# Gate and value of a GEGLU block by row parity: one block in three of the last sixty with one TensorE pass less, doubled even parts on ScalarE and sums on POOL

## Chip, cores, metric

One core of one Trainium2 chip. The metric is the device time of one execution in microseconds (us). A single-core program has no second die to compare with, so the state of a run is judged by its time against the fastest of the same kernel. Kernel times are medians. Where a ratio stands, it is the mean time of one kernel's fast runs over that of the other kernel's fast runs of the same rounds, so not quite the ratio of the medians that are quoted.

## The reference

```python
X = np.fft.fft(np.fft.fft(x, axis=1), axis=2).real        # x: 8 x 3008 x 256
x = X.reshape(24064, 256)
gelu = 0.5 * g * (1 + erf(g / sqrt(2)))   # g = x @ w_gate      (256 x 1536)
out  = (gelu * (x @ w_val)) @ w_out       #                     (1536 x 256)
```

Row t and row T - t of the transform are even and odd combinations of the same numbers. The kernel therefore holds an even part E and an odd part O for half the rows only, and makes "forward" rows from E + O and "mirrored" rows from E - O. The lowest odd channel is zero by nature; its place in O carries another number y, which belongs to the even side and needs a correction in the mirrored rows.

## The kernel before: the parts that matter

A *block* is one 128-wide slice of the hidden layer for up to 512 pairs of rows. There are 8 batches x 3 chunks x 12 slices = 288 blocks, numbered 0 to 287. Chunks have 512, 512 and 481 pairs. The last batch (252 to 287) has no later batch's transform beside it; its own is made beside blocks up to 249.

```python
def psum(tag):
    bufs = {"g": 2, "v": 3, "o": 1, "dft": 2}[tag]     # 8 banks in all
    return psum_pool.tile([128, 512], FP32, tag=tag, bufs=bufs, name=f"ps_{tag}")

# gate, forward rows: E + O, then GELU on ScalarE
mm(pg, n, "g", "E", fs, E, True, False)
mm(pg, n, "g", "O", fs, O, False, True)
nc.scalar.activation(gl[:, 0, :n], pg[:, :n], AF.Gelu)
# gate, mirrored rows, a block later: a third pass adds -2 O into the same bank
mm(pg, n, "g", "M", fs, O, False, True, skip_group_check=True)
nc.scalar.activation(_sub(gl, [[-1, n]], TOK + n - 1), pg[:, :n], AF.Gelu)

# value: two passes; VectorE keeps the even part (plus y * yw) before the second
mm(pv, n, "v", "E", fs, E, True, True)
nc.vector.scalar_tensor_tensor(ve[:, :n], EB_bufs[b][:, c0 : c0 + n],
    yw[:, fc : fc + 1], pv[:, :n], op0=ALU.mult, op1=ALU.add)
# ... a block later
mm(pv, n, "v", "O", fs, O, False, True, skip_group_check=True)
nc.vector.tensor_tensor(st["h"][:, fc, 0, :n], gl[:, 0, :n], pv[:, :n], op=ALU.mult)
nc.vector.scalar_tensor_tensor(_sub(vv, [[-1, n]], n - 1), ve[:, :n], 2.0, pv[:, :n],
    op0=ALU.mult, op1=ALU.subtract)                     # mirrored = 2 E' - (E + O)
nc.gpsimd.tensor_tensor(st["h"][:, fc, 1, :n], gl[:, 1, :n], vv[:, :n], op=ALU.mult)
# [...]
# per block, in every engine's queue in this order ("before" is the previous block):
parts["G"][fc]()                        # gate, forward
before[0]["g"][before[1]]()             # gate, mirrored
parts["V"][fc]()                        # value, even
two.pop(0)()                            # four output matmuls of the chunk before
before[0]["v"][before[1]]()             # value, odd, and the products
two.pop(0)()                            # four more; every third block ends with
                                        # ScalarE's copy of ps_o to out_sb
```

Two facts carry the whole argument: every engine takes its operations in the order of this listing (the traces below show a copy that is ready at 558.28 and starts at 559.08, behind a GELU queued ahead of it), and there are two gate banks and one output bank.

## Time and profile before

| | before |
|---|---|
| time, median (lowest to highest) | 629.23 us (628.73 to 629.72, 4 runs) |
| span of the profiled run | 627.0 us |
| busy: TensorE, VectorE, ScalarE, POOL | 98%, 92%, 68%, 81% |
| three blocks in the pure stretch (252 to 275, no transform work beside them) | 5.86 us |

In the profile PE is TensorE, PEld its weight loads, DVE VectorE, ACT ScalarE, and POOL the fourth compute engine. The prediction below shows the lines of the profile and how it reads them. In a line of the instructions in order of time the columns are start, duration, engine, source line, operation, output and inputs, shapes; in brackets stands the idle time of the engine just before, and whose end ended it. A matmul's recorded 0.38 us is its latency; its pace is 0.217.

### The profile page before, as it was taken

Reading aid. Unit: us, or ns where it says so; the run is one execution under the profiler, and the core shown is the slowest. Engines: PE = TensorE matmul, PEld = TensorE weight load, DVE = VectorE, ACT = ScalarE, POOL = GpSimd, SP = SyncE. Lnnn points to the kernel's source line nnn. Section 1 sums busy time; section 2 is a strip of 40 time slices with the busy share of each in tenths; the row PEclk is TensorE's granted clock in tenths of the full one; section 3 lists DMA queues with packets and bytes.
Section 4 is the critical chain, followed back from the end, with each engine's and each line's share of the span. In section 5 each row is a group of like instructions: output and inputs, shape, how many; then the busy total and the mean of one; then the engine's idle time right before and its main releaser. Section 6 shows DMA issues by size and latency. Waiting matters only on the chain.

```text
span 627.0 us, 12895 instructions
## 1 busy us (share of the span) xinstructions
PE 612.3 (98%) x4195; PEld 405.1 (65%) x4243; DVE 578.3 (92%) x941; ACT 428.4 (68%) x842; POOL 505.3 (81%) x510
## 2 busy tenths in 40 slices
PE   7999999999999999999999999999999999999997
PEld 3456666666666666666666666666666666666666
DVE  8689989999899999999999998999999999999992
ACT  6777677666776677667676677676676666666661
POOL 8399999989897998879997899969988655555651
PEclk8999999999999999999999999999999999999999
DMA  9961754536353353731645335633212322221123
GB/s 177 227 97 31 210 129 116 144 105 159 99 146 101 98 133 79 184 113 46 160 110 135 101 78 127 148 97 98 62 49 63 91 86 55 51 52 39 42 51 81
DMA packets 54217, 65.40 MB, mean 104 GB/s; under 512 B 7831, under 2 KB 49802, under 8 KB 51754
## 3 DMA queue, kind: packets, MB, share of 16 engines
q1 hardware_dynamic: 47222, 49.03, 30.6%
q0 software_dynamic: 6608, 15.29, 11.4%
q8 instruction: 33, 0.54, 0.4%
q10 hardware_dynamic: 320, 0.26, 0.2%
q14 instruction: 34, 0.28, 0.2%
HBM read 39.65 MB, written 30.17 MB: 111 GB/s over the span
## 4 chain that ended last, share of the span: by engine, by line
PE 93%; ACT 2%; issue 1%; DVE 1%; DMA 1%; POOL 1%; POOLq 0%; ACTq 0%
PE ps_o L749 38%; PE ps_g L660 28%; PE ps_v L660 19%; PE ps_dft L546 2%; PE ps_dft L582 2%; PE ps_o L820 1%; DMA Z_sb<-z 1%; PE ps_dft L443 1%; PE ps_dft L612 0%; ACT gelu_sb L676 0%; POOL h_sb L724 0%; POOL eo_sb L224 0%; DMA out_dram<-out_sb 0%; ACT gelu_sb L685 0%; PE ps_dft L749 0%
## 5 line engine op out<-in xcount | busy, mean ns | idle before, releaser
L724 POOL TENSOR_TENSOR h_sb<-gelu_sb,v_sb 128x512 bf16<-128x512 bf16 (+1 forms) x280 | 319.8, 1146 | 93.1 <-DVE v_sb L722 85.9
L749 PE MATMUL ps_o<-Wo_sb,h_sb 128*128 128x256 bf16 (+1 forms) x2232 | 334.9, 273 | 0.9 <-POOL h_sb L724 0.9
L749 PEld LDWEIGHTS <-h_sb 128*128 128x128 bf16 (+1 forms) x2304 | 228.7, 100 | 112.9 <-POOL h_sb L724 2.6
L676 ACT ACTIVATE gelu_sb<-ps_g 128x512 bf16<-128x512 f32 (+1 forms) x288 | 169.4, 588 | 98.6 <-PE ps_g L660 80.9
L660 PE MATMUL ps_g<-EO_sb,W_sb 128*128 128x512 bf16 (+1 forms) x817 | 228.5, 375 | 3.8 <-ACT gelu_sb L685 0.8
L704 DVE SCALAR_TENSOR_TENSOR ve_sb<-EB_sb,yw,ps_v 128x512 f32<-128x512 bf16 (+1 forms) x280 | 206.3, 737 | 25.9 <-PE ps_v L660 25.0
L660 PE MATMUL ps_v<-EO_sb,W_sb 128*128 128x512 bf16 (+1 forms) x575 | 213.7, 375 | 0.7 <-DVE W_sb L451 0.6
L720 DVE TENSOR_TENSOR h_sb<-gelu_sb,ps_v 128x512 bf16<-128x512 bf16 (+1 forms) x280 | 189.9, 678 | 1.1 <-ACT gelu_sb L685 0.7
L660 PEld LDWEIGHTS <-W_sb 128*128 128x128 bf16 x1440 | 137.2, 98 | 81.1 <-issue 1.8
L722 DVE SCALAR_TENSOR_TENSOR v_sb<-ve_sb,ps_v 128x512 f32<-128x512 f32 (+1 forms) x280 | 187.5, 670 | 0.0
L685 ACT ACTIVATE gelu_sb<-ps_g 128x512 bf16<-128x512 f32 (+1 forms) x288 | 168.7, 586 | 0.0
L769 ACT ACTIVATE out_sb<-ps_o 128x512 f32<-128x512 f32 x92 | 55.0, 598 | 35.7 <-PE ps_o L749 35.6
L224 POOL TENSOR_TENSOR eo_sb<-ab_sb 94x512 bf16<-94x512 f32 (+1 forms) x70 | 77.6, 1111 | 0.5
L549 ACT ACTIVATE S_sb<-ps_dft 96x512 bf16<-96x512 f32 x56 | 32.9, 588 | 14.0 <-PE ps_dft L546 13.9
L592 ACT ACTIVATE EO_sb<-ps_dft 128x512 bf16<-128x512 f32 (+1 forms) x44 | 26.0, 590 | 23.3 <-PE ps_dft L582 22.1
L217 POOL TENSOR_TENSOR ab_sb<-x_raw,x_raw 94x508 f32<-94x508 f32 (+1 forms) x30 | 33.0, 1100 | 0.0
L220 POOL TENSOR_TENSOR ab_sb<-x_raw,x_raw 94x508 f32<-94x508 f32 (+1 forms) x30 | 32.9, 1098 | 0.0
L546 PE MATMUL ps_dft<-eo_sb,G 94*96 94x256 bf16 x119 | 22.5, 274 | 0.2 <-POOL eo_sb L224 0.2
L158 POOL DMA_INDIRECT x_raw<-in_x_dram,idx x18 | 17.1, 948 | 2.9 <-issue 1.1
L582 PE MATMUL ps_dft<-TP,Z_sb 128*128 128x128 bf16 (+1 forms) x184 | 17.8, 218 | 0.0
L582 PEld LDWEIGHTS <-Z_sb 128*128 128x128 bf16 x192 | 14.6, 98 | 1.8 <-DVE Z_sb L534 0.6
L546 PEld LDWEIGHTS <-G 94*96 94x96 bf16 x119 | 13.0, 123 | 1.2 <-issue 0.4
(148 smaller groups left out, 166.2 us busy)
## 6 DMA issues: line engine op xcount, KB each, us to landing
out_dram<-out_sb SPq DMA_DIRECT2D x364, 64.0 KB
x_raw<-in_x_dram SPq DMA_DIRECT2D x10, 768.0 KB
Z_sb<-z SPq DMA_DIRECT2D x7, 768.0 KB
z<-S_sb SPq DMA_DIRECT2D x7, 576.0 KB
EB_sb<-yrow SPq DMA_DIRECT2D x14, 128.0 KB
z<-S_sb SPq DMA_DIRECT2D x7, 192.0 KB
x_raw<-in_x_dram SPq DMA_DIRECT2D x2, 640.0 KB
EB_sb<-yrow SPq DMA_DIRECT2D x7, 120.2 KB
```

The lines of the kernel that those rows point to most:

```text
L224: eng.tensor_tensor(_sub(eo, [[C, nj], [1, 128]], j0 * C + g * 128), ab(0, 0, [[1, 128]]), ab(1, 0, [[1, 128]]), op=op)
L546: nc.tensor.matmul(ps[:96, q * C : (q + 1) * C], G[:, j, :], _sub(eo, [[1, C]], j * C), start=(j == js[0]), stop=(j == js[-1]))
L582: nc.tensor.matmul(ps[:, o : o + n], st["Z"][:, pair, g * 128 : g * 128 + 128], _sub(TP, [[1, n]], g * 128), start=True, stop=True)
L660: nc.tensor.matmul(ps[:, :n], W[nm, part][:, fs], src, start=start, stop=stop, **kw)
L676: nc.scalar.activation(gl[:, 0, :n], pg[:, :n], AF.Gelu)
L685: nc.scalar.activation(_sub(gl, [[-1, n]], TOK + n - 1), pg[:, :n], AF.Gelu)
L704: nc.vector.scalar_tensor_tensor(ve[:, :n], EB_bufs[b][:, c0 : c0 + n], yw[:, fc : fc + 1], pv[:, :n], op0=ALU.mult, op1=ALU.add)
L720: nc.vector.tensor_tensor(st["h"][:, fc, 0, :n], gl[:, 0, :n], pv[:, :n], op=ALU.mult)
L722: nc.vector.scalar_tensor_tensor(_sub(vv, [[-1, n]], n - 1), ve[:, :n], 2.0, pv[:, :n], op0=ALU.mult, op1=ALU.subtract)
L724: nc.gpsimd.tensor_tensor(st["h"][:, fc, 1, :n], gl[:, 1, :n], vv[:, :n], op=ALU.mult)
L749: nc.tensor.matmul(pso[:m, half], st["h"][:, fc, sign, h0 : h0 + m], Wo_sb[:, fc, :], start=(fc == 0 and not (first and sign)), stop=(fc = ...
L769: nc.scalar.activation(_sub(osb, [[1, 2 * C]], 0, part_num=m), pso[:m, :], AF.Copy)
```

## The change

The intent: spare the third gate pass. In a treated block the gate is done like the value. ScalarE copies the doubled even part out of the bank before the odd pass is added, VectorE forms y * 2w - (E + O), POOL adds the two, and ScalarE takes GELU of that. The value half is changed too, because VectorE has no room for one more operation: its "keep the even part" is replaced by another doubling on ScalarE and another sum on POOL. Treated are blocks 229, 232, ... 283, which are 19.

```diff
+    APART = tuple(i for i in range(B * NS - 60, B * NS - 2) if i % 3 == 1)
 # l1_gate
+                if apart(ci, fc):
+                    mm(pg, n, "g", "E", fs, E, True, True)
+                    nc.scalar.activation(e2[:, :n], pg[:, :n], AF.Copy, scale=2.0)
+                    return
 # l1_gate_odd, new: queued behind the block's first four output matmuls
+                mm(pg, n, "g", "O", fs, O, False, True, skip_group_check=True)
+                nc.vector.scalar_tensor_tensor(
+                    d[:, :n], EB_bufs[b][:, c0 : c0 + n], ywg[:, fc : fc + 1], pg[:, :n],
+                    op0=ALU.mult, op1=ALU.subtract)
+                nc.scalar.activation(gl[:, 0, :n], pg[:, :n], AF.Gelu)
+                nc.gpsimd.tensor_tensor(d[:, :n], e2[:, :n], d[:, :n], op=ALU.add)
+                st["ps"][fc][0] = d
 # l1_gate2: the mirrored GELU reads d, without the third pass
 # l1_value
+                    nc.scalar.activation(e2[:, :n], pv[:, :n], AF.Copy, scale=2.0)
 # l1_value2
+                    nc.vector.scalar_tensor_tensor(
+                        _sub(vv, [[-1, n]], n - 1), EB_bufs[b][:, c0 : c0 + n],
+                        yw2[:, fc : fc + 1], pv[:, :n], op0=ALU.mult, op1=ALU.subtract)
+                    nc.gpsimd.tensor_tensor(vv[:, :n], _sub(ve, [[-1, n]], n - 1), vv[:, :n], op=ALU.add)
+                    nc.gpsimd.tensor_tensor(st["h"][:, fc, 1, :n], gl[:, 1, :n], vv[:, :n], op=ALU.mult)
 # make_ywg, new, in block 14: four small matmuls and copies, and
+        nc.vector.tensor_scalar(yw2, yw, 2.0, None, op0=ALU.mult)
 # [...]
```

More of the change, by code (lines that the diff above doesn't have):

```diff
@@ L135, in v_tile, with e2_tile @@
         return work([128, TOK], FP32, "v", 4, "v_sb")
+    def e2_tile():
+        return work([128, TOK], FP32, "e2", 2, "e2_sb")
     def osb_tile():
@@ L245 @@
     one_h = const_pool.tile([1, 1], BF16)
-    yw = const_pool.tile([128, NFC], FP32)
+    yw, yw2, ywg = (const_pool.tile([128, NFC], FP32, name=f"yw_{i}") for i in range(3))
     NGP = NJ * NK
@@ L477, in make_yw, with make_ywg @@
         return run
+    def make_ywg():
+        fcs = sorted({i % NFC for i in APART})
+        ps = psum("dft")
+        for fc in fcs:
+            nc.tensor.matmul(
+                ps[:, fc : fc + 1], W["g", "O"][0:1, fc * 128 : (fc + 1) * 128], one_h, start=True, stop=True)
+        for fc in fcs:
+            nc.scalar.activation(ywg[:, fc : fc + 1], ps[:, fc : fc + 1], AF.Copy, scale=2.0)
+        nc.vector.tensor_scalar(yw2, yw, 2.0, None, op0=ALU.mult)
     EO_bufs, EB_bufs = {}, {}
@@ L634, in tp_o @@
         return tp_e(b, gi, 1, engine)
+    NS = NG * NFC
+    APART = tuple(i for i in range(B * NS - 60, B * NS - 2) if i % 3 == 1)
     def store(b, gi, sub, sign, osb_half, queue):
@@ L667, in cols_of, with apart @@
             return n, c0, E, O, cstate[ci], slice(fc * 128, (fc + 1) * 128)
+        def apart(ci, fc):
+            return b * NS + ci * NFC + fc in APART
         def l1_gate(ci, fc):
@@ L672, in run @@
                 pg = psum("g")
+                if apart(ci, fc):
+                    mm(pg, n, "g", "E", fs, E, True, True)
+                    e2 = e2_tile()
+                    nc.scalar.activation(e2[:, :n], pg[:, :n], AF.Copy, scale=2.0)
+                    st["ps"][fc] = [pg, gelu_tile(), e2]
+                    return
                 mm(pg, n, "g", "E", fs, E, True, False)
@@ L678, in l1_gate, with l1_gate_odd, run @@
             return run
+        def l1_gate_odd(ci, fc):
+            def run():
+                if not apart(ci, fc):
+                    return
+                n, c0, _, O, st, fs = cols_of(ci, fc)
+                pg, gl, e2 = st["ps"][fc][:3]
+                del st["ps"][fc][2]
+                mm(pg, n, "g", "O", fs, O, False, True, skip_group_check=True)
+                d = v_tile()
+                nc.vector.scalar_tensor_tensor(
[4 more added lines that the diff above has]
+                st["ps"][fc][0] = d
+            return run
         def l1_gate2(ci, fc):
@@ L683, in run @@
                 pg, gl = st["ps"][fc][:2]
+                if apart(ci, fc):
+                    nc.scalar.activation(_sub(gl, [[-1, n]], TOK + n - 1), pg[:, :n], AF.Gelu)
+                    return
                 mm(pg, n, "g", "M", fs, O, False, True, skip_group_check=True)
@@ L702, in run @@
                 mm(pv, n, "v", "E", fs, E, True, True)
+                if apart(ci, fc):
+                    e2 = e2_tile()
+                    nc.scalar.activation(e2[:, :n], pv[:, :n], AF.Copy, scale=2.0)
+                    st["ps"][fc] += [pv, e2]
+                    return
                 ve = ve_tile()
@@ L711, in run @@
             def run():
-                n, _, _, O, st, fs = cols_of(ci, fc)
+                n, c0, _, O, st, fs = cols_of(ci, fc)
                 _, gl, pv, ve = st["ps"].pop(fc)
@@ L721, in run @@
                 vv = v_tile()
+                if apart(ci, fc):
+                    nc.vector.scalar_tensor_tensor(
+                        _sub(vv, [[-1, n]], n - 1), EB_bufs[b][:, c0 : c0 + n], yw2[:, fc : fc + 1], pv[:, :n],
+                        op0=ALU.mult, op1=ALU.subtract)
+                    nc.gpsimd.tensor_tensor(vv[:, :n], _sub(ve, [[-1, n]], n - 1), vv[:, :n], op=ALU.add)
+                    nc.gpsimd.tensor_tensor(st["h"][:, fc, 1, :n], gl[:, 1, :n], vv[:, :n], op=ALU.mult)
+                    return
                 nc.vector.scalar_tensor_tensor(
@@ L777, in ffn_work @@
             parts = {k: [f(ci, fc) for fc in range(NFC)] for k, f in (
-                ("G", l1_gate), ("V", l1_value), ("g", l1_gate2), ("v", l1_value2))}
+                ("G", l1_gate), ("O", l1_gate_odd), ("V", l1_value), ("g", l1_gate2), ("v", l1_value2))}
             subs = [nsub - 1, *range(nsub - 1)] if last(ci) else range(nsub)
@@ L874, in behind_first_gate @@
         tp_y(0, 0)()
-    NS = NG * NFC
     def plan():
@@ L894, in plan @@
             at(fill, s, f)
+        at(fill, 14, make_ywg)
         for i, f in enumerate(early):
@@ L972, in feed @@
                 two.pop(0)()
+            parts["O"][fc]()
             for f in pool.pop(i, []):
```

## The prediction

> **What bounds the kernel now.** I read the page's engine totals first, then its chain that ended last, then busy time in stretches, then the instructions in order of time for the last batch, where the change acts. Totals and chain:
>
> ```profile
> PE 612.3 (98%) x4195; PEld 405.1 (65%) x4243; DVE 578.3 (92%) x941; ACT 428.4 (68%) x842; POOL 505.3 (81%) x510
> ...
> PE 93%; ACT 2%; issue 1%; DVE 1%; DMA 1%; POOL 1%; POOLq 0%; ACTq 0%
> ```
>
> TensorE carries 93% of the chain, but VectorE is 92% busy, so it matters which really has room. The stretches (columns: PE, PEld, DVE, ACT, POOL busy; clock; DMA) show VectorE busy for all of 560 to 580 while POOL is busy for 58%:
>
> ```profile
> 500.00:520.00 20.00, 19.89 (x137) 12.97 (x138) 19.28 (x30) 13.67 (x27) 11.64 (x10) 1.00 0.31 90
> ...
> 560.00:580.00 20.00, 19.89 (x134) 13.38 (x135) 20.00 (x32) 12.79 (x26) 11.67 (x10) 1.00 0.18 44
> ```
>
> One block (one 128-wide slice of the hidden layer for 512 mirrored pairs of rows) in order of time:
>
> ```profile
> 561.18 0.81 PE L660 MATMUL ps_g<-EO_sb,W_sb 128*128 128x512 bf16 x3
> 561.62 0.68 DVE L722 SCALAR_TENSOR_TENSOR v_sb<-ve_sb,ps_v 128x512 f32<-128x512 f32 x1
> 561.83 0.38 PE L660 MATMUL ps_v<-EO_sb,W_sb 128*128 128x512 bf16 x1
> ...
> 561.88 0.60 ACT L676 ACTIVATE gelu_sb<-ps_g 128x512 bf16<-128x512 f32 x1 [0.87 <-PE ps_g L660]
> ...
> 562.25 0.75 DVE L704 SCALAR_TENSOR_TENSOR ve_sb<-EB_sb,yw,ps_v 128x512 f32<-128x512 bf16 x1
> 562.37 0.59 ACT L685 ACTIVATE gelu_sb<-ps_g 128x512 bf16<-128x512 f32 x1
> ...
> 562.45 1.17 POOL L724 TENSOR_TENSOR h_sb<-gelu_sb,v_sb 128x512 bf16<-128x512 bf16 x1 [0.79 <-DVE v_sb L722]
> 562.48 0.38 PE L660 MATMUL ps_v<-EO_sb,W_sb 128*128 128x512 bf16 x1
> ...
> 562.97 0.69 DVE L720 TENSOR_TENSOR h_sb<-gelu_sb,ps_v 128x512 bf16<-128x512 bf16 x1
> 563.03 0.64 PEld L660 LDWEIGHTS <-W_sb 128*128 128x128 bf16 x4
> 563.14 0.81 PE L660 MATMUL ps_g<-EO_sb,W_sb 128*128 128x512 bf16 x3
> ```
>
> The period is 563.14 - 561.18 = 1.96 us. In the chain a first-layer pass costs 0.217 (three gate passes 0.65) and four output matmuls 0.44: 5 x 0.217 + 0.87 = 1.96. TensorE has no gap: it sets the pace. VectorE's three durations (0.75 + 0.69 + 0.68 = 2.12) exceed the period because neighbours overlap in the record. What they cost back to back shows at 125 us, where VectorE catches up after a wait:
>
> ```profile
> 125.96 0.74 DVE L704 SCALAR_TENSOR_TENSOR ve_sb<-EB_sb,yw,ps_v 128x512 f32<-128x512 bf16 x1
> 126.61 0.68 DVE L720 TENSOR_TENSOR h_sb<-gelu_sb,ps_v 128x512 bf16<-128x512 bf16 x1
> 127.21 0.68 DVE L722 SCALAR_TENSOR_TENSOR v_sb<-ve_sb,ps_v 128x512 f32<-128x512 f32 x1
> 127.81 0.75 DVE L704 SCALAR_TENSOR_TENSOR ve_sb<-EB_sb,yw,ps_v 128x512 f32<-128x512 bf16 x1
> ```
>
> Start to start: 0.65 + 0.60 + 0.60 = 1.85, so VectorE has only 0.1 us of room per block. POOL's multiply is 1.17 long, 1.12 start to start when queued; its sums of two f32 tiles in the fold take longer:
>
> ```profile
> L724 POOL TENSOR_TENSOR h_sb<-gelu_sb,v_sb 128x512 bf16<-128x512 bf16 x184 | 213.9, 1166 | 66.2 <-DVE v_sb L722 59.9 <-ACT gelu_sb L676 4.1 <-ACT S_sb L549 1.0
> ...
> L217 POOL TENSOR_TENSOR ab_sb<-x_raw,x_raw 94x508 f32<-94x508 f32 x24 | 30.3, 1264 | 0.0
> ```
>
> **What the Trainium skill says.** "Perfetto Trace Analysis" (section Identifying the Most-Contended Engine) warns that matmul busy time does not measure distance to the limit because matmuls are pipelined, while occupancy is fair for VectorE. Here the first half holds (0.38 recorded against 0.217 of pace); for VectorE the trace differs, 100% occupancy against 1.85 of 1.96 us needed. "GPSIMD Engine Reference", section 3.1, gives about 2.6 cycles per element for a two-input elementwise operation; its 4497 ns for 2048 f32 elements scales to an estimate of 1.12 us for 512, and the trace has 1.17 to 1.26. "PSUM — Partial Sum Buffer", section Specifications, lets POOL read no PSUM, which is why ScalarE must copy the even parts out; the trace has no POOL reader of ps. The same page, section PSUM bank collisions raise a hardware error, forbids two engines in one bank and partition at once, two readers included. In the changed program the forward GELU does wait for VectorE's read of the same gate bank; before, only ScalarE read gate banks, so no row shows it yet.
>
> **The change, part by part.** Blocks 229, 232, ... 283 are treated: 19 of 288. Call three neighbours A (treated), B, C.
> Removed in A: one gate pass, 0.217 of TensorE. If all were gain: 19 x 0.217 = 4.1 us.
> Added to ScalarE: two doublings, each like the out_sb copy (0.60, 0.49 start to start). Per three blocks it then has 9 operations x 0.49 = 4.4 of 5.87 us: room by sum.
> VectorE swaps one operation: the ve form leaves, two of that form (pointer scalar, bf16 input, PSUM) stand where one ve and one immediate-scalar form stood. A: 0.65 + 0.60 + 0.65 = 1.90; three blocks 1.90 + 2 x 1.85 = 5.60. Fits.
> POOL: two f32 sums more. Three blocks: 3 x 1.12 + 2 x 1.24 = 5.84 against 5.87 now and 5.65 aimed at. So the sum of POOL alone eats nearly the whole gain.
> Setup: four one-column matmuls, four copies like yw's (0.18 us) and a small VectorE doubling in block 14: +0.2.
>
> Then the order. Reading the changed program's queues, a ring closes from one A to the next A'. Let S be the end of POOL's gate sum in A.
> ScalarE: mirrored GELU of A from S + 0.10, then the out_sb copy queued behind it from + 0.59 to + 1.19. There is one ps_o buffer, so TensorE's next output matmuls in C wait for that copy, to S + 1.25. Then 0.44 + 0.22 + 0.44 to the first gate pass of A': S + 2.34. (The other way round, ScalarE's GELU of C and the mirrored one of B must free the gate bank: about S + 2.2, nearly the same.)
> In A': result of the even pass + 0.38 + 0.10 of latency (as PE end 561.78 to ACT 561.88), doubling 0.60, so the odd pass, which accumulates into the bank being copied, starts 1.15 after the even one; + 0.38 + 0.04 to VectorE: S + 3.91. VectorE 0.75, hand-over to POOL 0.14 (562.30 to 562.45 above), sum 1.26: S + 6.06.
> So the ring alone needs 6.06 for three blocks that now take 5.87.
> POOL's in-order queue adds to it: after S it does C0's multiply (1.12), then the value sum of A, which waits for VectorE's mirrored row, 3.85 + 0.14 after the gate subtraction started. With period P that is S + 3.91 - P + 3.99. Then 1.22 + 1.12 + 1.12 + 1.26. P = (7.90 - P) + 4.72 gives P = 6.31 as the mean of an alternation between 6.06 and 6.56.
>
> Sum by stretch, three-block periods from the VectorE starts: blocks 229 to 240, where the last batch's transforms still interleave, take 6.17 now (512 columns): + 0.14 x 4 = 0.6. Blocks 241 to 252 (481 columns, transforms) 5.98 now, and the ring scaled by about 0.95 is 6.0: 0.0. Blocks 253 to 276, pure, 5.87: + 0.44 x 8 = 3.5. Blocks 277 to 285, pure, 481 columns, 5.68: + 0.3 x 3 = 0.9. Together + 5.0; setup + 0.2; minus 0.3 because the first period starts with empty queues and minus 0.2 for the last A, behind which no ring closes. 629.7 + 4.7 = 634.4.
>
> **Rivals.** (1) TensorE stays the bound and the pass is gained: 625.6. For it: the chain is TensorE's, ScalarE and POOL show room in the totals. Against: the two hand-overs inside one gate bank, and POOL's sum. (2) POOL's throughput bounds without further waits: 5.84 against 5.87 in the pure stretch, more PE work elsewhere, some passes gained where transforms interleave: about 629. For it: 4 v buffers and 5 gelu buffers let engines slide. Against: one ps_o and two ps_g buffers do not. (3) VectorE becomes the bound: 5.60 is below 5.65, and would cost nothing; it needs its operations some 5% dearer. (4) The ring runs at its upper value 6.56 throughout, for instance when f32 sums of 128 partitions beside ScalarE are slower: 8 x 0.69 + 3 x 0.5 + 4 x 0.4 = 8.6, about 638.5.
>
> **Range and chances.** The ring is built of trace durations, but its hand-over times are taken from other pairs of engines, and slack in one buffer that I read too strictly brings rival 2. I put 55% on the ring, 30% on rival 2, 10% on rival 1, 5% on rival 4 or worse; weighted a little towards the rivals below, I keep 634.0, and 627.0 to 640.0 holds 8 in 10. Over 2% faster (below 617) would need three times the removed work: 0.01. Over 2% slower (above 642): 0.03. Within: 0.96.
>
> **What would show it.** The first-layer matmul count falls by 19, with four tiny ones added. Right: TensorE's busy share falls in 500 to 610 and gaps appear before its output matmuls released by ScalarE's out_sb copy, and before gate passes released by GELU; ScalarE waits for the POOL sum before the mirrored GELU of A; POOL is over 90% busy there with the value sum waiting for VectorE; three blocks take over 5.9 us in 545 to 588. Wrong: three blocks near 5.65 (rival 1) or near 5.84 with POOL gapless (rival 2), POOL sums near 1.0 us, or VectorE gapless with longer operations (rival 3).

## The result, and the profile after

The changed kernel takes 638.2 us (636.72 to 638.55, 4 runs) against 629.23: ratio 1.0138, 95% interval 1.0119 to 1.0158, some 9 us slower. The page of the changed kernel answers to the two lines that the prediction showed of before:

```profile
PE 616.5 (97%) x4228; PEld 404.5 (64%) x4228; DVE 577.0 (91%) x942; ACT 447.0 (70%) x884; POOL 549.0 (86%) x548
...
PE 84%; ACT 4%; DVE 3%; issue 3%; DMA 2%; POOL 2%; SPq 1%; ACTq 0%; DVEq 0%; POOLq 0%
```

The totals of TensorE and VectorE hardly move; the second line does. It is the chain of work that ended last, followed back from the last instruction, and TensorE's share of it falls from 93% to 84%. The weight loads fall from 4243 to 4228: 19 taken away, four small ones added. (The matmul count rises from 4195 to 4228, because records of matmuls are missing from a trace, more from the first one; it can't be used for this.) Busy time in the pure stretch, first before, then after (columns: PE, PEld, DVE, ACT, POOL busy with counts; clock; DMA share; GB/s):

```profile
545.00:588.00 43.00, 42.73 (x283) 28.36 (x286) 43.00 (x67) 27.33 (x52) 25.55 (x23) 1.00 0.19 45
```
```profile
545.00:588.00 43.00, 39.71 (x263) 25.83 (x262) 39.48 (x63) 32.61 (x63) 39.70 (x35) 1.00 0.20 43
```

POOL goes from 59% to 92%, and TensorE and VectorE lose 3.0 and 3.5 us of work in the same 43: each of the three is busy for 92%, none for all of it, which fits a ring of waits. Here is one turn of it in the changed kernel, in order of time (L721 is POOL's gate sum, L730 the mirrored GELU of the treated block, L829 the output copy, L698 the doubling, L717 VectorE's gate subtraction, L720 the forward GELU, L779 POOL's value sum, L780 and L784 POOL's multiplies):

```profile
557.24 1.27 POOL L721 TENSOR_TENSOR v_sb<-e_sb,v_sb 128x512 f32<-128x512 f32 x1
...
557.68 0.60 PE L809 MATMUL ps_o<-Wo_sb,h_sb 128*128 128x256 bf16 x4
...
558.54 0.63 ACT L730 ACTIVATE gelu_sb<-v_sb 128x512 bf16<-128x512 f32 x1 [0.75 <-POOL v_sb L721]
...
559.08 0.58 ACT L829 ACTIVATE out_sb<-ps_o 128x512 f32<-128x512 f32 x1
...
559.71 0.60 PE L809 MATMUL ps_o<-Wo_sb,h_sb 128*128 128x256 bf16 x4 [0.57 <-ACT out_sb L829]
...
559.93 1.27 POOL L779 TENSOR_TENSOR v_sb<-e_sb,v_sb 128x512 f32<-128x512 f32 x1 [0.30 <-DVE v_sb L776]
...
560.79 0.60 PE L679 MATMUL ps_g<-EO_sb,W_sb 128*128 128x512 bf16 x2
561.21 0.60 ACT L698 ACTIVATE e_sb<-ps_g 128x512 f32<-128x512 f32 x1 [0.58 <-PE ps_g L679]
...
561.27 1.16 POOL L780 TENSOR_TENSOR h_sb<-gelu_sb,v_sb 128x512 bf16<-128x512 bf16 x1
...
561.88 0.38 PE L679 MATMUL ps_g<-EO_sb,W_sb 128*128 128x512 bf16 x1
...
562.30 0.75 DVE L717 SCALAR_TENSOR_TENSOR v_sb<-EB_sb,yw,ps_g 128x512 f32<-128x512 bf16 x1 [0.38 <-PE ps_g L679]
...
562.40 1.16 POOL L784 TENSOR_TENSOR h_sb<-gelu_sb,v_sb 128x512 bf16<-128x512 bf16 x1
...
563.51 1.28 POOL L721 TENSOR_TENSOR v_sb<-e_sb,v_sb 128x512 f32<-128x512 f32 x1
```

Read it with S = 558.51, the end of the first gate sum. The last output matmuls for the copy L829 end at 558.28 on record (557.68 plus 0.60), but ScalarE stood before L730 until POOL's sum came, so the copy began at 559.08. The output matmuls restart at S + 1.20 (the prediction said 1.25), the even gate pass of the next treated block at S + 2.28 (2.34), VectorE's subtraction at S + 3.79 (3.91). The next gate sum could have followed VectorE's end at 563.05; it starts at 563.51, when POOL is through with its multiplies (L780, L784), which stood behind the value sum. That is the part of POOL's queue in the ring. The turn took 6.27 us; the eight turns of the stretch take 6.27 to 6.39, 6.33 in the mean.

Where the 9 us came from: I numbered VectorE's forward products (one per block) in both traces and subtracted. The lag of the changed kernel behind before, in us:

| at block | 8 | 28 | 227 | 239 | 251 | 275 | 287 |
|---|---|---|---|---|---|---|---|
| lag | 1.01 | 1.69 | 1.99 | 3.24 | 4.64 | 8.28 | 9.29 |

So 7.30 us arise in the treated stretch and 1.99 before it, of which 1.01 is there at block 8, ahead of the first changed instruction.

### The profile page after: what moved, and what is told of

It is laid out like the page before. It is cut to its first block, busy times and chain, and to the rows that moved or that the text cites. A ratio compares the mean times of both kernels' runs of the same rounds, so it can differ in the third digit from the quotient of the medians.

```text
span 636.3 us, 12995 instructions
## 1 busy us (share of the span) xinstructions
PE 616.5 (97%) x4228; PEld 404.5 (64%) x4228; DVE 577.0 (91%) x942; ACT 447.0 (70%) x884; POOL 549.0 (86%) x548
## 4 chain that ended last, share of the span: by engine, by line
PE 84%; ACT 4%; DVE 3%; issue 3%; DMA 2%; POOL 2%; SPq 1%; ACTq 0%; DVEq 0%; POOLq 0%
PE ps_o L809 35%; PE ps_g L679 26%; PE ps_v L679 17%; PE ps_dft L560 2%; ACT out_sb L829 2%; PE ps_dft L596 1%; PE ps_o L880 1%; DMA EO_sb<-yrow 1%; DMA out_dram<-out_sb 1%; POOL v_sb L721 1%; DMA Z_sb<-z 1%; DVE h_sb L773 1%; DVE v_sb L782 1%; POOL h_sb L784 1%; ACT gelu_sb L704 1%
## 5 line engine op out<-in xcount | busy, mean ns | idle before, releaser
L784 POOL TENSOR_TENSOR h_sb<-gelu_sb,v_sb 128x512 bf16<-128x512 bf16 (+1 forms) x261 | 298.0, 1146 | 47.6 <-DVE v_sb L782 44.0
L757 DVE SCALAR_TENSOR_TENSOR ve_sb<-EB_sb,yw,ps_v 128x512 f32<-128x512 bf16 (+1 forms) x261 | 192.1, 736 | 23.6 <-PE ps_v L679 22.3
L704 ACT ACTIVATE gelu_sb<-ps_g 128x512 bf16<-128x512 f32 (+1 forms) x269 | 158.0, 588 | 71.4 <-PE ps_g L679 68.6
L679 PEld LDWEIGHTS <-W_sb 128*128 128x128 bf16 x1421 | 135.3, 97 | 78.1 <-issue 2.7
L782 DVE SCALAR_TENSOR_TENSOR v_sb<-ve_sb,ps_v 128x512 f32<-128x512 f32 (+1 forms) x261 | 174.7, 670 | 0.0
L733 ACT ACTIVATE gelu_sb<-ps_g 128x512 bf16<-128x512 f32 (+1 forms) x269 | 157.8, 586 | 0.0
L829 ACT ACTIVATE out_sb<-ps_o 128x512 f32<-128x512 f32 x92 | 54.6, 594 | 27.4 <-PE ps_o L809 27.4
L779 POOL TENSOR_TENSOR v_sb<-e_sb,v_sb 128x512 f32<-128x512 f32 (+1 forms) x19 | 22.5, 1183 | 7.5 <-DVE v_sb L776 6.2
L721 POOL TENSOR_TENSOR v_sb<-e_sb,v_sb 128x512 f32<-128x512 f32 (+1 forms) x19 | 23.8, 1250 | 1.3 <-DVE v_sb L717 1.2
L780 POOL TENSOR_TENSOR h_sb<-gelu_sb,v_sb 128x512 bf16<-128x512 bf16 (+1 forms) x19 | 21.7, 1144 | 1.5
L717 DVE SCALAR_TENSOR_TENSOR v_sb<-EB_sb,yw,ps_g 128x512 f32<-128x512 bf16 (+1 forms) x19 | 14.0, 737 | 8.9 <-PE ps_g L679 8.0
```

What stands on the lines that cost most here:

```text
L679: nc.tensor.matmul(ps[:, :n], W[nm, part][:, fs], src, start=start, stop=stop, **kw)
L829: nc.scalar.activation(_sub(osb, [[1, 2 * C]], 0, part_num=m), pso[:m, :], AF.Copy)
```

## The experiments

Theory (the ring): the loss is a chain of hand-overs from one treated block to the next, through ScalarE's queue and the few PSUM banks, which POOL's queue lengthens. Rivals: POOL's load as such; VectorE; the setup in block 14. Each run took place beside runs of the kernel before on the same chip; the chip differs between e1 to e4, e5 to e8, e9 to e11 and e12, so times are compared by their ratios. "Lag" below is the growth of the lag from block 227 to 287, read as above from one trace of each kernel; "three blocks" is 5.86 us plus an eighth of its growth from 251 to 275.

| run | time, median | ratio to before (95%) | lag 227 to 287 | three blocks |
|---|---|---|---|---|
| the change | 638.2 | 1.0138 (1.0119 to 1.0158) | 7.30 | 6.32 |
| e1_setup | 630.55 | 1.0008 (0.9995 to 1.0021) | 0.15 | 5.88 |
| e2_setup_act | 637.57 | 1.0120 (1.0098 to 1.0142) | 7.33 | 6.32 |
| e3_value_only | 629.72 | 0.9993 (0.9976 to 1.0010) | 0.21 | 5.86 |
| e4_gate_only | 635.28 | 1.0083 (1.0069 to 1.0098) | 4.89 | 6.21 |
| e5_sum_aside (wrong result) | 629.22 | 0.9985 (0.9965 to 1.0005) | -0.09 | 5.79 |
| e6_two_o | 636.57 | 1.0107 (1.0089 to 1.0126) | 6.78 | 6.25 |
| e7_late | 632.14 | 1.0035 (1.0019 to 1.0052) | 2.56 | 6.06 |
| e8_later | 631.84 | 1.0033 (1.0013 to 1.0054) | 2.43 | 6.04 |
| e9_six | 630.59 | 1.0011 (0.9993 to 1.0030) | 0.99 | - |
| e10_later_four | 637.06 | 1.0102 (1.0084 to 1.0120) | 6.43 | - |
| e11_later_six | 630.34 | 1.0006 (0.9989 to 1.0022) | 0.88 | - |
| e12_behind_six | 627.84 | 0.9955 (0.9931 to 0.9979) | -2.01 | - |

### e1_setup: the setup by itself

```diff
         def apart(ci, fc):
-            return b * NS + ci * NFC + fc in APART
+            return False
```

> Setup alone: the four weight columns are made and doubled in block 14, no block is treated. My record gave it +0.2 us. Theory A (blocked doubling): the small VectorE doubling, 128x12, took 2.26 us in the changed kernel and ended as two queued POOL operations ended (55.81), so it cost VectorE about 2 us where VectorE is the busy engine; then this kernel is 1.0 to 2.2 us slower than before and the doubling is again over 1 us long. Rival B: the 2.0 us lead lost by block 158 in the changed kernel's profile was the chance of the opening (1.0 of it is there before block 14); then within 0.5 us of before.

In the changed kernel (instructions of VectorE and POOL in order of time):

```profile
53.55 1.16 POOL L784 TENSOR_TENSOR h_sb<-gelu_sb,v_sb 128x512 bf16<-128x512 bf16 x1
...
53.58 2.26 DVE L491 TENSOR_SCALAR yw<-yw 128x12 f32<-128x12 f32 x1
...
54.67 1.14 POOL L223 TENSOR_TENSOR ab_sb<-xb 94x508 f32<-94x508 bf16 x1
```

Twelve columns take VectorE 2.26 us, and they end (55.84) as the second POOL operation ends (55.81). The doubling was 1.85 us long again in this run. But the kernel is only 0.5 us slower than before, interval -0.3 to 1.3: in its trace the lag steps up by 1.8 us from block 13 to block 14, and nothing of that is left at block 27. The following blocks made the stall up. Expectation A was too high. It still is more than the 0.2 us, by its mean.

### e2_setup_act: the same change, doubling on ScalarE

```diff
-        nc.vector.tensor_scalar(yw2, yw, 2.0, None, op0=ALU.mult)
+        nc.scalar.activation(yw2, yw, AF.Copy, scale=2.0)
```

> The full change, but the doubling of the value columns is done by ScalarE instead of VectorE; same result. Theory A: 1.0 to 2.0 us faster than the changed kernel, so 7 to 8 us slower than before (ratio about 1.012), and no small operation of 2 us on VectorE. Rival B: no difference to the changed kernel beyond 0.5 us (ratio 1.014).

637.57 us, ratio 1.0120 where the change had 1.0138; the two intervals overlap, so the 1.1 us between them is not established. In the trace the step of the lag at block 14 is 0.5 us here and 2.2 in the change. The lag in the treated stretch is the same (7.33 against 7.30), so the setup has no part in it. This kernel is the base of all further runs. Its six times spread from 635.7 to 640.9, and its profiled run had already 2.86 us of lag at block 8. Over the profiled runs that lag runs from -0.45 to 2.86, without any changed instruction ahead of it: the opening varies by itself, and a single profile can't settle a microsecond there.

### e3_value_only and e4_gate_only: the halves

```diff
 # e3_value_only: l1_gate, l1_gate_odd, l1_gate2 as before
-                if apart(ci, fc):
+                if False:
 # e4_gate_only: l1_value, l1_value2 as before, by the same edit there
```

> Only the value half of the change (ScalarE doubles, POOL sums, VectorE one short form less); the gate keeps three TensorE passes; setup on ScalarE. TensorE work is as before, POOL has 4 operations in three blocks (4.6 us), no hand-over stands in a gate bank. Ring theory: the loss comes from the gate half, so this is within 1.0 us of before, three blocks at 5.87 in the pure stretch. Rival (POOL or ScalarE load as such slows everything): 2 to 4 us slower.

Measured: equal to before, three blocks 5.86. ScalarE's doublings and POOL's value sums cost nothing here, where no gate bank is handed around.

> Only the gate half (one TensorE pass less in a treated block, gate sum on POOL); the value half as before; setup on ScalarE. VectorE then needs 0.65 + 0.65 + 0.60 + 0.60 = 2.50 in the treated block and 6.20 in three; POOL has 4 operations (4.6). Ring theory with VectorE's sum: three blocks at 6.2 to 6.3 in the pure stretch, total 5 to 8 us slower than before. Rival (POOL's throughput was the bound of the changed kernel): POOL is now free, three blocks near 5.65 to 5.87 and the total equal to before or faster.

Measured: 5.3 us slower by the medians of the rounds, three blocks 6.21. VectorE's sum had said 6.20, worked out from start-to-start times, and VectorE is busy for 43.00 of the 43 us from 545 to 588 (39.48 in the change). POOL has four operations in three blocks here and waits; its throughput is not needed for a loss. The waits of this kernel from 500 to 610 us (who waited for whom: total, times, longest) name VectorE too (L717 and the GELU L720 read the same gate bank):

```profile
ACT gelu_sb L720 <- DVE v_sb L717: 17.6, 18, 1.1
```

The two losses of the halves do not add to that of the whole (0 and 4.9 against 7.3): as these readings have it, the gate half is bound by VectorE when alone, and by the ring with POOL's queue when the value half relieves VectorE.

### e5_sum_aside: POOL's work kept, but taken out of the ring

```diff
-                nc.gpsimd.tensor_tensor(d[:, :n], e2[:, :n], d[:, :n], op=ALU.add)
+                nc.gpsimd.tensor_tensor(e2[:, :n], e2[:, :n], d[:, :n], op=ALU.add)
```

> Wrong result on purpose: POOL still forms the gate sum, with the same operands, but into a tile that nobody reads; the mirrored GELU of a treated block reads VectorE's result directly. POOL's load is as in the changed kernel (3 x 1.12 + 1.24 + 1.35 = 5.95 for three blocks), and its gate sum no longer stands between VectorE and ScalarE. Setup on ScalarE as in e2_setup_act, which is the comparison. Ring theory: three blocks fall from 6.33 to 5.95 or less in the pure stretch, total 1 to 2 us above before. Rival (POOL's load as such makes the 6.33): unchanged, 7 to 8 us above before.

The result is wrong (relative error 0.21). The time is that of before, some 8 us less than e2_setup_act, though POOL executes every operation. Now POOL is without a gap, with two gate sums 5.95 us apart, as its sum had said:

```profile
560.64 1.27 POOL L721 TENSOR_TENSOR e_sb<-e_sb,v_sb 128x512 f32<-128x512 f32 x1
...
566.59 1.27 POOL L721 TENSOR_TENSOR e_sb<-e_sb,v_sb 128x512 f32<-128x512 f32 x1
```

POOL as a load makes at most 5.95; what makes 6.33 is the place of its sum between VectorE and ScalarE. The rival falls. (The lag, read at VectorE's products, gives 5.79 for the same stretch: POOL falls behind the other engines there.) Without the wait the change gains nothing either, though 19 passes are saved; POOL's 5.95 is above the 5.86 of before, which would explain it, but no run tried that. The time is what the prediction's rival 2 named (about 629).

### e6_two_o: a second bank for the output

```diff
-                        st["pso"][sub] = psum("o")
+                        st["pso"][sub] = psum("dft" if b == B - 1 and sub % 2 else "o")
```

> Correct result: in the last batch the output matmuls alternate between two PSUM banks (one of the transform banks is idle there), so that TensorE need not wait for the copy of the previous output rows. Reading the waits alone, 11 of 19 treated blocks lose their 0.4 to 0.5 us each: 4 us faster than e2_setup_act. Ring theory: behind that wait stands the gate bank, freed by the mirrored GELU of the next block about 0.1 us earlier, so the ring shrinks by 0.14 and the period by half of it: 0.8 us faster than e2_setup_act at most, three blocks 6.2 to 6.3, and the wait reappears at the even gate pass.

A reader of the changed kernel's waits would start here: TensorE waits 7.5 us in all for the output copy. The edit reaches only part of them: the output matmuls of the last batch begin at block 264, and the second bank is first written at 576.39 us, in block 267. TensorE's waits from 490 to 615 us:

```profile
PE ps_o L809 <- ACT out_sb L829: 4.3, 9, 0.9
PE ps_g L679 <- ACT gelu_sb L733: 2.7, 6, 0.6
```

All nine records of the first line lie before 574 us, where there is still one bank, as in the changed kernel (4.3 us in nine records there too). Behind that no wait for the copy is left; six waits for the gate bank, 2.7 us, stand where e2_setup_act has seven for the copy, 3.4 us. The treated stretch gains 0.55 us against e2_setup_act by lag, practically all of it behind block 263. There the gate sums are 6.27 apart in the mean where e2_setup_act has 6.33; half of 0.14 less was expected (the table's 6.25 mixes blocks with one and with two banks). The ratio falls by 0.0013, inside the noise. So of 3.4 us of waits that were taken away some 0.5 was gained; the 4 us of the plain reading were never within this edit's reach.

### e7_late and e8_later: another order for ScalarE

```diff
 # the mirrored GELU of a treated block, and POOL's multiply behind it, leave
 # l1_gate2 and l1_value2 for a step of their own, l1_late
+                nc.scalar.activation(_sub(gl, [[-1, n]], TOK + n - 1), d[:, :n], AF.Gelu)
+                nc.gpsimd.tensor_tensor(st["h"][:, fc, 1, :n], gl[:, 1, :n], vv[:, :n], op=ALU.mult)
 # e7_late: called at the end of the next block (behind the output copy)
 # e8_later: called in the second next block, behind its parts["G"]
```

> Correct result: the mirrored GELU of a treated block and POOL's multiply behind it are issued at the end of the next block, behind the copy of the output rows instead of ahead of it. Ring theory: ScalarE's copy no longer waits for POOL's gate sum, the ring is about 0.6 shorter, three blocks about 6.05 (from the same balance with POOL's queue), so about 5 us faster than e2_setup_act and 2 to 3 us slower than before. Rival POOL load: no change to e2_setup_act.

> Correct result: the same two operations one step later still, behind the forward GELU of the second next block. Ring theory: only the mirrored GELU of the next block is left behind the gate sum; POOL's queue alone then sets 5.95 for three blocks, total 0.5 to 2 us slower than before, never faster by over 1 us. Rival POOL load: as e2_setup_act. Rival VectorE: 5.60 needed, so no bound.

Nothing is added or removed but the place of two operations. e7_late loses 2.2 us instead of 7.6, three blocks 6.06 where 6.05 was expected: most of the change's loss goes when the output copy no longer waits behind a GELU that waits for POOL. In its trace TensorE has no wait for the copy left from 490 to 630 us, and 3.1 us for the gate bank. (POOL's multiply moved along with the GELU; the two moves were not tried apart.) e8_later is no better, a little worse than expected. Its POOL is nearly without a gap at 6.04 (5.95 expected), and TensorE still waits for the gate bank, 3.2 us in all. Both results stand against the load as the only cause, but in e8_later load and ring can't be told apart.

### e9_six, e10_later_four, e11_later_six: fewer treated blocks

```diff
-    APART = tuple(i for i in range(B * NS - 60, B * NS - 2) if i % 3 == 1)
+    APART = tuple(i for i in range(B * NS - 60, B * NS - 2) if i % 6 == 1)   # % 4 == 1 in e10_later_four
 # e10_later_four and e11_later_six: with the late order of e8_later
```

> The full change in every sixth block instead of every third (10 blocks), order as in the change, setup on ScalarE, correct result. POOL has 6 x 1.12 + 2.59 = 9.3 of some 11.6 us, so it is far from full. Ring theory: each treated block still costs, since from an even gate pass at 0 the gate sum ends at 3.72 at best, the output copy behind it at 4.91, and TensorE wanted its bank at 4.62: 0.35 lost against 0.22 saved, so 0.13 x 10 = 1.3 us slower than before, with TensorE waits for the output copy in most of the ten. Rival POOL load: no loss left, 10 x 0.22 = 2 us faster than before.

> Every fourth block, with the mirrored GELU and its multiply issued late as in e8_later, setup on ScalarE, correct result. POOL needs 4 x 1.12 + 2.59 + 0.1 = 7.2 in four blocks that TensorE does in 7.61, VectorE 7.45. Ring theory: nothing waits on the ring, so 14 or 15 treated blocks gain 0.15 to 0.2 each: 1.5 to 2.5 us faster than before (about 627.5 to 628.5 against 629.7). Wrong if it is not faster than before.

> As e10_later_four, but every sixth block (10 blocks). Ring theory: 1.0 to 2.0 us faster than before, and 2.5 to 3 us faster than e9_six, which differs from it in nothing but the place of two operations in the queues. If it equals e9_six, the order of issue was not the cause.

e9_six: 0.7 us slower by the ratio, interval -0.4 to 1.9; the lag of 0.99 is 0.10 per treated block, where 0.13 was worked out. With POOL far from full, a pass saved still earns nothing. TensorE waits for the output copy, 1.5 us in seven records.

e10_later_four missed badly: 6.4 us slower by the ratio, where 1.5 to 2.5 us faster was expected. The lag by blocks shows how: it jumps by 0.7 to 1.0 us right after blocks 233, 245, 257, 269 and 281, five of its treated blocks, all with number 2 modulo 3. The other ten cost some 0.1 us each, like the ten of e11_later_six below. The output copy comes every third block; the change treats blocks 1 modulo 3 only, one in four treats all three kinds. In block 257 (instructions in order of time; L720 the forward GELU of the treated block, L839 the output copy):

```profile
557.59 0.60 ACT L720 ACTIVATE gelu_sb<-ps_g 128x512 bf16<-128x512 f32 x1 [0.29 <-DVE v_sb L717]
...
558.09 0.59 ACT L839 ACTIVATE out_sb<-ps_o 128x512 f32<-128x512 f32 x1
...
558.73 0.60 PE L819 MATMUL ps_o<-Wo_sb,h_sb 128*128 128x256 bf16 x4 [0.66 <-ACT out_sb L839]
```

Here the copy falls behind the treated block's own forward GELU, which waits for VectorE's turn in the gate bank, and TensorE's next output matmuls wait for the copy. The queue position of one copy is worth more than the pass. (This is read from the trace; no run moved the copy.) I had looked at each engine's sum and not at that phase.

e11_later_six missed as well: as e9_six within the noise, though the output copy is out of the way. Its trace says why. In a block two after a treated one (L742 is the late GELU, L733 the mirrored GELU of the block between):

```profile
584.51 0.62 ACT L742 ACTIVATE gelu_sb<-v_sb 128x512 bf16<-128x512 f32 x1
...
585.03 0.59 ACT L733 ACTIVATE gelu_sb<-ps_g 128x512 bf16<-128x512 f32 x1
...
585.67 0.59 PE L679 MATMUL ps_g<-EO_sb,W_sb 128*128 128x512 bf16 x2 [0.23 <-ACT gelu_sb L733]
```

The gate pass of the next block needs the bank that L733 reads. TensorE's work before it ends at 585.28 (584.84 plus 0.44 for four output matmuls), so it loses 0.39, and the late GELU ahead of L733 took 0.5 of ScalarE's time. One wait had been moved to the other bank.

### e12_behind_six: one place further back

```diff
 # against e11_later_six
             parts["G"][fc]()
-            if older:
-                older[0]["L"][older[1]]()
             if before:
                 before[0]["g"][before[1]]()
+            if older:
+                older[0]["L"][older[1]]()
             parts["V"][fc]()
```

> As e11_later_six (ten blocks, setup on ScalarE, correct result), with the mirrored GELU of the treated block one place later still: behind the mirrored GELU of the next block, not ahead of it. In the trace of e11_later_six TensorE's even gate pass waits 0.39 us three blocks after each treated one, until that next block's mirrored GELU has freed the gate bank (585.62 to 585.67), and the late GELU ahead of it is 0.5 long. Theory (a chain over the two gate banks through ScalarE's order): this wait goes, each treated block keeps most of its 0.22, and the ten give 1.5 to 2.2 us: 627.5 to 628.5 against 629.7, the lead to before over blocks 227 to 287 falls by as much. Rival (the treated block costs something else, such as its own odd pass or VectorE): as e11_later_six, 0 to 0.5 us slower than before.

627.84 us, ratio 0.9955, interval 0.9931 to 0.9979: faster than before by 2.3 us of the medians, and than the change by about 10 (which ran in other rounds). The lag falls by 2.01 us over ten treated blocks, 0.20 each: practically the whole pass. The same place in this trace:

```profile
584.26 0.59 ACT L733 ACTIVATE gelu_sb<-ps_g 128x512 bf16<-128x512 f32 x1
...
584.74 0.63 ACT L742 ACTIVATE gelu_sb<-v_sb 128x512 bf16<-128x512 f32 x1
...
585.03 0.81 PE L679 MATMUL ps_g<-EO_sb,W_sb 128*128 128x512 bf16 x3
```

L733 comes first, the bank is free at 584.85, and TensorE passes without a bracket. The result is correct. Its interval is clear of 1. (One run of before in these rounds took 634.3 us; without it the gap of the means is 2.2 us.)

## Why the prediction was right, and where a term was off

The direction, the size and the cause were on record: slower by under 2%, through a ring, not through an engine's sum. 638.2 lies inside 627 to 640, though 4 us above the value given: the loss is 9.0 us where 4.7 had been worked out. It is close to the 638.5 of rival 4, whose ring of 6.56 did not come about. Step by step:

- *What bounds before*: e3_value_only and e12_behind_six fit TensorE as the pace. One pass less, with nothing waiting, is worth 0.20 of its 0.217.
- *VectorE's sum*: confirmed to 0.01 in e4_gate_only (6.21 against 6.20), and both new forms last 0.74 to 0.75, as taken from the ve form. Rival 3 did not come true in the change itself.
- *POOL's sum*: 1.24 start to start was right for the gate sum. The value sum is 1.35. The multiply behind it reads what it wrote, which may be the reason; it follows in every trace, so no run shows it. That 0.11 was missing, and three blocks need 5.95, not 5.84 (e5_sum_aside).
- *The ring*: each point of it was found within 0.12 us of where the working put it, and the period of the pure stretch is 6.33 against 6.31. In part that is luck, since two errors cancel: VectorE's subtraction comes at S + 3.79 instead of 3.91, and POOL's four operations from the value sum to the end of the gate sum take 4.86 (559.93 to 564.79) instead of 4.72. POOL's value sum starts 4.01 behind VectorE's gate subtraction (555.92 to 559.93), where 3.99 was worked out. With these terms the balance gives (3.79 + 4.01 + 4.86) / 2 = 6.33. Of the alternation between 6.06 and 6.56 there is a small one, 6.27 to 6.30 and 6.37 to 6.39 in turn: any two neighbours add to 12.64 to 12.67 where the balance said 12.62, so the balance fits and only the swing was put too wide.
- *The wait in brackets*: that the output bank and the gate bank stand one behind the other (S + 2.34 and S + 2.2) was on record, and e6_two_o showed it where its second bank is in use.
- *The mis-sized term* is the sum by stretch. Pure stretch + 3.5: measured + 3.64. Last stretch + 0.9: + 1.01. But blocks 229 to 240 were put at + 0.6 and gave + 1.25, blocks 241 to 252 at 0.0 and gave + 1.40. Together 2.0 us of the missing 4. I had set the ring's 6.31 against the longer period of these blocks as if the transforms' work ran beside the ring. (One of these periods was misread besides: VectorE's starts in before give 6.10 for blocks 229 to 240, not 6.17, so the same working would have given + 0.8.) The gate sums of blocks 229 to 240 are 6.21 to 6.71 apart, mostly more than in the pure stretch. That the transforms' copies on ScalarE and matmuls on TensorE are part of the ring's own queues would explain it; no run took them out, so that is argued, not shown.
- *Setup and ends*: setup + 0.2, measured + 0.5 with an interval that holds 0.2. The 0.5 taken off for the first and last turn does not show in the lag. About 1 us of lag from the opening stays open.
- *The signs promised*: copies and GELU ahead of TensorE's gaps, ScalarE waiting for the POOL sum (10.7 us in all), POOL over 90%, over 5.9 us for three blocks: all there. The matmul count was no usable sign; the weight loads were.

What the prediction lacked was a remedy, and my first two failed for the same reason that the change did: e10_later_four and e11_later_six were worked out from engine sums plus the one wait I was looking at.

## What to carry to other kernels

Before moving work from the busiest engine to idle ones, write down the loop of hand-overs that the move closes, with in-order queues and bank counts, and compare its length with the time it must fit in: here 6.3 us against 5.86, while every engine's sum was worked out to fit (POOL's, measured, is 5.95, a tenth of a us too long). When a wait shows, ask what stands in the same queue behind and ahead of it; taking the named wait away alone (e6_two_o) gave some 0.5 us for 3.4 us of waits, and moving one GELU behind the one that frees a bank (e12_behind_six against e11_later_six) turned no gain into 2.3 us.

## What the Trainium skill lacked or had wrong

- "SBUF — State Buffer", section Who interferes with whom, names tensor_scalar among the VectorE operations that can take the port pair shared with POOL: "Whoever issues first gets the shared pair for the whole instruction". The 128x12 doubling fits it, at 2.26 us in the change and 1.85 in e1_setup. What the page lacks: in both it ended only with a second POOL operation, which had started after it (54.67 against 53.58 in the change), which suggests that a queue of POOL work can hold VectorE for longer than one instruction. This is read from two traces and was not tried apart.
- "GPSIMD Engine Reference", section 3.1: its 4497 ns for 2048 elements scales to an estimate of 1.12 us for 512; the f32 sums here took 1.27 us of record and 1.24 start to start, and 1.35 where the next POOL operation reads the result. The page has no figure for the second case.
- No page gives the hand-over from VectorE's end to POOL's start: 0.14 us here (a subtraction ending at 562.30 in before, the POOL multiply at 562.45).
